# Moving operand sums, layer norm, an output projection and softmax reductions in a fused attention and gated-MLP kernel

## The chip, the cores and the metric

The kernel runs on one core of one Trainium2 chip. A core has five engines with a queue each: TensorE (PE in the profile, with its weight loads as PEld), VectorE (DVE), ScalarE (ACT), GpSimd (POOL) and SyncE (SP, used here only to issue loads). Each engine takes its instructions strictly in the order of its queue, and semaphores tie the engines together. The metric is the device time of one execution in microseconds (us); smaller is better.

## What is computed

For a sequence of 2048 rows of width 1024, with 32 heads of 32, a window of 8 keys at a distance of 2 rows each, and an inner MLP width of 3584:

```python
xn = layernorm(x)                                  # over the 1024 columns, no weights
q, k, v = split(xn @ wqkv)                         # 32 heads of 32
logits[s, w] = q[s] . k[s - 2 w] * 32 ** -0.5      # w = 0..7, masked where s - 2 w < 0
o[s] = sum_w softmax_w(logits)[s, w] * v[s - 2 w]
s = o @ wo
g = silu((silu(xn @ w1) * (xn @ w3)) @ w2)
out = x + s * g
```

Inputs and output are bfloat16.

## The kernel before, in words

The sequence is cut into four chunks of 512 rows (c = 0..3) and two blocks of two chunks (b = 0, 1). For a block the program says, in this order: the q, k, v projection of the first chunk (`qkv`), four sums of the block's normed input (`xn_sums`), most of the MLP's first half (`mlp_up`), the attention of the first chunk, `qkv` of the second chunk, the rest of `mlp_up`, the attention of the second chunk, and `down_wo` (the MLP's second half, with the layer norm of the next block's chunks in its middle, and the output projection `wo` of both chunks at its end).

**Products by seven instead of eight.** The MLP's products are done as 2x2 block products with seven multiplications (a Strassen-Winograd scheme), so operands must be added and subtracted first. `mlp_up` runs over 14 steps (`fb`, 256 columns of w1 and w3 each), and a step has seven products for each of two 128-column halves, of 4 matmuls each: 56 matmuls of 128x512. The weight sums of a step (`st`, lines 289 to 292) are made by VectorE in block 0, written to DRAM (`s_dram`, line 293) and only loaded again in block 1. Likewise the sums of w2's four quarters (`w2_sums`, lines 346 to 355) are made once, written to `t_dram`, and loaded in `down_wo`. Before, all 14 `w2_sums` are said ahead of `mlp_up(0)`; they work in place, in the two halves of the space of the second chunk's q (`qo[:, 1]`), which is free until `qkv(1)`.

**Inside a step of `mlp_up`** the order of products is a11 (into `ua`), s1 (into `ue`), a12, s2 (into `ub`), s4 (into `ue`), s3 (into `ub`), and last a22 into `ub`, which is put off as `tail` and issued behind the next step's first two products. VectorE adds `ue` to a saved sum (line 327) and `ub` to another (line 332); line 332 reads the bank `ub` into which the tail then accumulates, so the tail's matmuls wait for it. Lines 340 and 343 multiply up and gate.

**Who sets the order.** The kernel is written with a framework that takes the program order as priority, works out each engine's queue ahead of time with a model of how long everything takes, and puts in all semaphores. `tc.high_priority()` lifts instructions above the others. So VectorE's queue is a fixed mixture of operand sums, evacuations of PSUM and pieces of attention; whatever stands in front must finish (or get its data) before what is behind can start. Pools hand out buffers by tag: `r8` has six buffers of 8 KiB per partition, which hold the x tiles, the weight tiles `wt`, the sums `st` and `wot`; `att` three; `k2` eight; PSUM eight banks.

**Attention of a chunk** is all on VectorE but the exponential: 8 x (two products of q and shifted k, lines 210 to 214), a rearranging transfer by 16 DMAs of POOL's queue (line 218), three additions, maximum, subtraction, exponential, sum, reciprocal, product (lines 222 to 235), a rearranging transfer back (line 238), then 16 products with shifted v and 14 additions (lines 246 to 261), which leave the result in `qo`. A halo of 16 columns of kT and vT is copied by POOL at the start of the next `qkv` (lines 182 and 183), and only then may the new k and v be written.

**`down_wo`** does seven products of 4 x 14 matmuls, with operand sums on VectorE in place (lines 396, 397, 406, 417). The layer norm of the next block's chunks (`ln_norm`, lines 139 to 156, VectorE statistics with the square root on ScalarE) and its transposes on TensorE (`ln_tp`) stand between its products (lines 435 and 444). The gate `gt` lies in the memory of `xs`. At the end the output projections of both chunks follow, 64 matmuls each; VectorE evacuates each bank by lines 469 and 470 without priority.

Of the kernel before, what the change touches and what calls it, by code (L numbers as in the profile page):

```python
# [16 lines left out]
def kernel(  # L17
# [106 lines left out]
    def bank(name):  # L124
        return psum.tile([P, CH], FP32, tag="mm", name=name)
# [31 lines left out]

    def ln_tp(c, st, xt4):
        for kh in range(2):
            tp = bank(f"tp{c}_{st}_{kh}")  # L160
            for k in range(KH):
                kt = kh * KH + k
                nc.tensor.matmul(
                    tp[:, k * P:(k + 1) * P], lhsT=xt4[:, st, kt * P:(kt + 1) * P], rhs=ident[:],
                    start=(k == 0), stop=(k == KH - 1), skip_group_check=True,
                )
            nc.scalar.copy(
                out=xT[:, c % 2, kh * KH:(kh + 1) * KH, st * P:(st + 1) * P],
                in_=tp[:].rearrange("p (k t) -> p k t", k=KH),
            )  # L170
# [31 lines left out]

    def attention(c):
# [23 lines left out]
        mx = small.tile([P, P], FP32, tag="mx", bufs=1)  # L227
        nc.vector.tensor_reduce(out=mx[:], in_=z[:].rearrange("p w s -> p s w"), axis=AX.X, op=ALU.max)
        nc.vector.tensor_sub(z[:], z[:], mx[:].unsqueeze(1).to_broadcast([P, W, P]))
        nc.scalar.activation(out=z[:], in_=z[:], func=ACTF.Exp, scale=scale)  # L230
        ssum = small.tile([P, P], FP32, tag="ssum", bufs=1)
        nc.vector.tensor_reduce(out=ssum[:], in_=z[:].rearrange("p w s -> p s w"), axis=AX.X, op=ALU.add)
        nc.vector.reciprocal(out=ssum[:], in_=ssum[:])
        pb = att.tile([P, W, P], BF16, tag="a4", name=f"pb{c}")
        nc.vector.tensor_mul(pb[:], z[:], ssum[:].unsqueeze(1).to_broadcast([P, W, P]))  # L235
# [27 lines left out]
    def xn_sums():  # L263

        k_1, k_2 = slice(0, KH), slice(KH, KT)
        nc.vector.tensor_sub(xs[:, 0], xT[:, 1, k_1, :], xT[:, 0, k_1, :])
        nc.vector.tensor_sub(xs[:, 1], xT[:, 1, k_2, :], xs[:, 0])
        nc.vector.tensor_sub(xs[:, 2], xT[:, 1, k_2, :], xT[:, 1, k_1, :])
        nc.vector.tensor_sub(xs[:, 3], xT[:, 0, k_2, :], xs[:, 1])
# [10 lines left out]

    def mlp_up(b, fbs):
        for fb in fbs:
            fc = slice(fb * 256, (fb + 1) * 256)
            wt = r8.tile([P, 2, KT, 2 * P], BF16, tag="r8")
            st = r8.tile([P, 4, KH, 2 * P], FP16, tag="r8")
            nc.sync.dma_start(out=wt[:, 0], in_=w1_r[:, :, fc])
            if b == 0:
                nc.sync.dma_start(out=wt[:, 1], in_=w3_r[:, :, fc])
                nc.vector.tensor_add(st[:, 0], wt[:, 1, 0:KH], wt[:, 1, KH:KT])  # L289
                nc.vector.tensor_sub(st[:, 1], st[:, 0], wt[:, 0, 0:KH])  # L290
                nc.vector.tensor_sub(st[:, 2], wt[:, 0, 0:KH], wt[:, 1, 0:KH])
                nc.vector.tensor_sub(st[:, 3], wt[:, 0, KH:KT], st[:, 1])  # L292
                nc.gpsimd.dma_start(out=s_dram[fb], in_=st[:])  # L293
            else:
                nc.sync.dma_start(out=st[:], in_=s_dram[fb])
                nc.sync.dma_start(out=wt[:, 1, KH:KT], in_=w3_r[:, KH:KT, fc])
# [27 lines left out]
            for i in I:  # L324
                mm_prod(pe[i], s4[i], b22, False)
                with hp():
                    nc.vector.tensor_add(su2[i][:], pe[i][:], su2[i][:])
            sg2 = []
            for i in I:
                mm_prod(pb[i], s3[i], t3, False)  # L330
                with hp():
                    nc.vector.tensor_add(h_sb[:, fl[i], CH:BL], pb[i][:], sp5[i][:])  # L332
                    sg2.append(k2.tile([P, CH], BF16, tag="k2", name=f"sg2{b}_{fl[i]}"))
                    nc.scalar.activation(out=sg2[i][:], in_=su2[i][:], func=ACTF.Silu)

# [9 lines left out]

    def w2_sums(i):

        bq = qo[:, 1].rearrange("p (u q) n -> p u q n", u=2)[:, i % 2]
        tq = bq.bitcast(FP16)
        nc.sync.dma_start(out=bq.rearrange("p (a c) n -> p a c n", a=2), in_=w2_q[:, i])  # L350
        nc.vector.tensor_sub(tq[:, 0], bq[:, 1], bq[:, 0])  # L351
        nc.vector.tensor_sub(tq[:, 1], bq[:, 3], bq[:, 1])
        nc.vector.tensor_sub(tq[:, 3], bq[:, 3], tq[:, 0])
        nc.vector.tensor_sub(tq[:, 2], bq[:, 2], tq[:, 3])  # L354
        nc.gpsimd.dma_start(out=t_dram[:, i], in_=tq)  # L355

    T1, T3, T4, T2 = range(4)

    def down_wo(b):
# [20 lines left out]
        def hA(row, fh):  # L380
            return [[h_sb[:, fh * FH + k, gsl[row][g]] for k in range(FH)] for g in G]
# [6 lines left out]
        gt = [xsb[:, 2 * u:2 * u + 2].rearrange("p a k n -> p (a k) n") for u in range(2)]  # L388
# [6 lines left out]
        for g in G:  # L395
            nc.vector.tensor_add(s1t[g], a21[g], a22[g])
            nc.vector.tensor_sub(s3t[g], a11[g], a21[g])
        rhs = rhs_tiles("w", 0, 0)
        lhs = hA(0, 0)
# [4 lines left out]
        for g in G:  # L404
            pb.append(fork(f"db{b}_{g}", pa[g]))
            nc.vector.tensor_sub(s2t[g], s1t[g], a11[g])
# [9 lines left out]
        for g in G:  # L416
            nc.vector.tensor_sub(s4t[g], a12[g], s2t[g])
# [16 lines left out]
        if b + 1 < NB:  # L434
            ln_transpose(2 * b + 2)
# [7 lines left out]
        if b + 1 < NB:  # L443
            ln_transpose(2 * b + 3)
# [7 lines left out]
        wots = []  # L452
        for dh in range(2):
            wot = r8.tile([P, NJ, CH], BF16, tag="r8")
            nc.sync.dma_start(out=wot[:], in_=wo_r[:, :, dh * CH:(dh + 1) * CH])
            wots.append(wot)
        for u in range(2):
            c = 2 * b + u
            for dh in range(2):
                cols = slice(dh * CH, (dh + 1) * CH)  # L460
                for st in range(NST):
                    g0 = (c * NST + st) * P
                    ps = bank(f"s{c}_{dh}_{st}")
                    mm_prod(ps, [qo[:, u, j, st * P:(st + 1) * P] for j in range(NJ)],
                            [wots[dh][:, j, :] for j in range(NJ)], True)
                    x_e = k2.tile([P, 2, CH], BF16, tag="k2")
                    nc.sync.dma_start(out=x_e[:, 0], in_=x_flat[g0:g0 + P, cols])
                    o_t = k2.tile([P, CH], FP32, tag="k2")
                    nc.vector.tensor_mul(o_t[:], ps[:], gt[u][:, dh * NST + st])
                    nc.vector.tensor_add(x_e[:, 1], o_t[:], x_e[:, 0])  # L470
                    nc.scalar.dma_start(out=out_flat[g0:g0 + P, cols], in_=x_e[:, 1])

    cut = (12, 10)
    ln_transpose(0, group=1)
    ln_transpose(1)
    for b in range(NB):
        c0, c1 = 2 * b, 2 * b + 1
        qkv(c0)
        xn_sums()
        if b == 0:  # L480
            for i in range(FH):
                w2_sums(i)
# [7 lines left out]
        down_wo(b)  # L490
# [30 lines left out]
```

## Time and profile before

| | |
|---|---|
| median of 3 runs | 811.35 us (808.3 to 812.58) |
| the profiled execution, whole | 811.54 us |
| its span, first to last instruction | 809.8 us |
| instructions in it | 9377 |
| granted TensorE clock, mean | 0.972 |
| DMA | 146.37 MB, 181 GB/s on average |

The profile is of one execution, so it explains 811.54 us, which is 0.02% from the median. Between the span and the whole lie 1.74 us. TensorE counts as busy while a matmul is in its pipe, so 94% busy does not say that it runs at its peak; that has to be worked out from the number of matmuls and the time of one. The granted clock is a share of full speed, and falls after an idle time.

### The profile page before, as it was taken

Reading aid. Unit: us, or ns where it says so; the run is one execution under the profiler, and the core shown is the slowest. Engines: PE = TensorE matmul, PEld = TensorE weight load, DVE = VectorE, ACT = ScalarE, POOL = GpSimd, SP = SyncE. Lnnn points to the kernel's source line nnn. Section 1 sums busy time; section 2 is a strip of 40 time slices with the busy share of each in tenths; the row PEclk is TensorE's granted clock in tenths of the full one; section 3 lists DMA queues with packets and bytes.
Section 4 is the critical chain, followed back from the end, with each engine's and each line's share of the span. In section 5 each row is a group of like instructions: output and inputs, shape, how many; then the busy total and the mean of one; then the engine's idle time right before and its main releaser. Section 6 shows DMA issues by size and latency. Waiting matters only on the chain.

```text
span 809.8 us, 9377 instructions
## 1 busy us (share of the span) xinstructions
PE 757.9 (94%) x3516; PEld 378.2 (47%) x3516; DVE 621.8 (77%) x845; ACT 291.7 (36%) x494; POOL 122.5 (15%) x172
## 2 busy tenths in 40 slices
PE   5998679999999799996969999999999999999997
PEld 2664234444456444443424664444446644444443
DVE  7458789857779999585798389584895895955976
ACT  4333234435533241227300334565443345311200
POOL 0011010221400503904000000404000004040000
PEclk7999799999999999998988999999999999999999
DMA  9687785666752545565726443847553438465423
GB/s 331 239 285 247 257 263 196 188 168 216 217 199 75 174 152 171 171 170 147 255 91 194 170 151 128 229 131 202 187 175 124 137 136 224 160 177 181 130 64 119
DMA packets 118958, 146.37 MB, mean 181 GB/s; under 512 B 6016, under 2 KB 93568, under 8 KB 115328
## 3 DMA queue, kind: packets, MB, share of 16 engines
q1 hardware_dynamic: 106176, 111.16, 43.7%
q0 software_dynamic: 8128, 30.42, 11.4%
q10 hardware_dynamic: 4608, 4.20, 1.5%
q8 instruction: 27, 0.44, 0.2%
q14 instruction: 19, 0.16, 0.1%
HBM read 111.15 MB, written 26.21 MB: 170 GB/s over the span
## 4 chain that ended last, share of the span: by engine, by line
PE 61%; DVE 20%; DMA 10%; issue 4%; ACT 2%; POOL 2%; SPq 0%; DVEq 0%; POOLq 0%
DMA qo<-in_B_w_dram 4%; DMA wt<-in_B_w_dram 4%; DVE p_t L210 2%; DVE stats L148 2%; DVE B L246 1%; DVE C L246 1%; DVE B L260 1%; POOL vT L183 1%; DVE qo L261 1%; PE db_3_5573 L119 1%; PE db_2_5570 L119 1%; PE db_1_5567 L119 1%; PE db_0_5564 L119 1%; DVE h_sb L332 1%; DMA L_1_2424<-E 1%
## 5 line engine op out<-in xcount | busy, mean ns | idle before, releaser
L119 PEld LDWEIGHTS <-wt 128*128 128x128 bf16 x1440 | 176.7, 123 | 163.7 <-issue 33.8
L119 PEld LDWEIGHTS <-st 128*128 128x128 f16 x896 | 87.7, 98 | 106.1 <-issue 0.5
L119 PEld LDWEIGHTS <-h_sb 128*128 128x128 bf16 (+1 forms) x672 | 65.8, 98 | 78.2 <-issue 1.1
L210 DVE TENSOR_TENSOR p_t<-qo,kT 128x2048 bf16<-128x2048 bf16 x64 | 77.1, 1216 | 27.0 <-ACT kT L201 27.0
L119 PEld LDWEIGHTS <-qo 128*128 128x128 bf16 x256 | 25.7, 100 | 40.4 <-issue 11.7
L212 DVE TENSOR_TENSOR p_t<-p_t 128x2048 bf16<-128x2048 bf16 x32 | 38.9, 1215 | 0.0
L246 DVE TENSOR_TENSOR B<-E,vT 128x2048 bf16<-128x2048 bf16 x32 | 38.6, 1216 | 0.0
L182 POOL COPY kT<-kT 128x128 bf16<-128x128 bf16 x3 | 19.0, 6325 | 122.6 <-DVE p_t L210 122.6
L183 POOL COPY vT<-vT 128x128 bf16<-128x128 bf16 x3 | 13.4, 4471 | 150.0 <-DVE C L246 150.0
L261 DVE TENSOR_TENSOR qo<-qo,B 128x2048 bf16<-128x2048 bf16 x24 | 29.2, 1217 | 0.2
L260 DVE TENSOR_TENSOR B<-B,C 128x2048 bf16<-128x2048 bf16 x24 | 29.2, 1216 | 0.1
L246 DVE TENSOR_TENSOR C<-E,vT 128x2048 bf16<-128x2048 bf16 x24 | 29.2, 1216 | 0.0
L351 DVE TENSOR_TENSOR qo<-qo 128x512 f16<-128x512 bf16 x14 | 5.9, 422 | 28.2 <-DMA qo<-in_B_w_dram 28.2
L470 DVE TENSOR_TENSOR x_e<-o_t,x_e 128x512 bf16<-128x512 f32 x32 | 21.7, 687 | 3.3 <-DMA x_e<-in_A_x_dram 2.8
L355 POOL DMA_DIRECT2D t_dram<-qo x14 | 7.6, 546 | 95.4 <-DVE qo L354 85.1
L213 DVE TENSOR_TENSOR p_t<-p_t 128x1024 bf16<-128x1024 bf16 x32 | 21.9, 684 | 0.2
L293 POOL DMA_DIRECT2D s_dram<-st x14 | 7.6, 544 | 76.5 <-DVE st L292 67.4
L246 DVE TENSOR_TENSOR qo<-E,vT 128x2048 bf16<-128x2048 bf16 x8 | 9.7, 1216 | 9.9 <-DMA E<-pb_5430 9.9
L119 PEld LDWEIGHTS <-xT 128*128 128x128 f16 x112 | 10.9, 98 | 13.2
L289 DVE TENSOR_TENSOR st<-wt 128x1024 f16<-128x1024 bf16 x14 | 9.6, 685 | 9.8 <-DMA wt<-in_B_w_dram 9.8
L201 ACT CAST qo<-qkv_0_0_3418 128x512 bf16<-128x512 f32 x1 | 0.6, 586 | 39.9 <-DMA out_dram<-x_e 39.9
L238 POOL DMA_DIRECT2D E<-pb_5430 x16 | 9.2, 580 | 32.3 <-DVE pb_5430 L235 30.6
(1312 smaller groups left out, 1598.1 us busy)
## 6 DMA issues: line engine op xcount, KB each, us to landing
wt<-in_A_wqkv_dram SPq DMA_DIRECT2D x24, 1024.0 KB, 5.8
wt<-in_B_w_dram SPq DMA_DIRECT2D x42, 512.0 KB, 4.8
s_dram<-st POOLq DMA_DIRECT2D x14, 1024.0 KB, 7.1
wt<-t_dram SPq DMA_DIRECT2D x16, 896.0 KB, 5.3
st<-s_dram SPq DMA_DIRECT2D x14, 1024.0 KB, 5.6
wt<-in_B_w_dram SPq DMA_DIRECT2D x12, 896.0 KB, 5.2
qo<-in_B_w_dram SPq DMA_DIRECT2D x14, 512.0 KB, 4.6
t_dram<-qo POOLq DMA_DIRECT2D x14, 512.0 KB, 4.0
```

The costliest lines, as they stand in the source:

```text
L119: nc.tensor.matmul(ps[:], lhsT=lhs[k], rhs=rhs[k], start=(first and k == 0), stop=(k == n - 1), skip_group_check=not first,)
L148: nc.vector.bn_stats(out=stats[:, h, :], in_=xt4[:, st, h * 512:(h + 1) * 512])
L182: nc.gpsimd.tensor_copy(out=kT[:, :, 0:HALO], in_=kT[:, :, CH:CH + HALO])
L183: nc.gpsimd.tensor_copy(out=vT[:, :, 0:HALO], in_=vT[:, :, CH:CH + HALO])
L210: nc.vector.tensor_mul(p_t[:], qT[:, jh * 4:jh * 4 + 4, :], kT[:, jh * 4:jh * 4 + 4, o:o + CH])
L212: nc.vector.tensor_add(pr[0][:], pr[0][:], pr[1][:])
L213: nc.vector.tensor_add(pr[0][:, 0:2, :], pr[0][:, 0:2, :], pr[0][:, 2:4, :])
L246: nc.vector.tensor_mul(dst, E[:, w, :].unsqueeze(1).to_broadcast([P, 4, CH]), vT[:, js, o:o + CH])
L260: nc.vector.tensor_add(B[:], B[:], C[:])
L261: nc.vector.tensor_add(A, A, B[:])
L289: nc.vector.tensor_add(st[:, 0], wt[:, 1, 0:KH], wt[:, 1, KH:KT])
L470: nc.vector.tensor_add(x_e[:, 1], o_t[:], x_e[:, 0])
```

## The change

- `mlp_up` loads the tiles of step fb + 1 before the matmuls of step fb (`up_load`). In block 0 the weight sums of step fb + 1 (`w_sums`) are queued on VectorE behind step fb's second line-327 addition ("m"), by an ordering constraint (`tc.issue_after`).
- `w2_sums(fb)` moves into step fb of block 0, queued behind that step's last line-332 addition ("t"); its quarters are loaded a step earlier (`w2_load`), into one buffer of the pool `r8` instead of q's space.
- The layer norm of chunks 2 and 3 is said at the start of `mlp_down` and runs on ScalarE (`ln_norm_act`: mean by a copy with accumulation, sum of squares, root, then scale and shift), except for two tiny VectorE instructions. The transposes stay between the same products.
- `wo` becomes a function of one chunk. A block's second `wo` comes behind the `qkv` of the next block's first chunk (at the end, behind the first `wo`). It loads its weights for each chunk. Its evacuations get priority.
- The maximum and the sum over the 8 window positions become trees of three pairwise operations.
- `xn_sums` and the operand sums of the down half get priority, and block 0's first part has 11 steps instead of 12.

```diff
+    def ln_norm_act(c, sts, xt4):
+        n = len(sts)
+        v = small.tile([P, 4, n], FP32, tag="v")
+        for i, st in enumerate(sts):
...
+            nc.sync.dma_start(out=x_t, in_=x_flat[g * P:(g + 1) * P, :])
+            junk = k2.tile([P, D], BF16, tag="k2", name=f"junk{c}_{st}")
+            nc.scalar.activation(out=junk[:], in_=x_t, func=ACTF.Copy, scale=-1.0 / D, accum_out=v[:, 0, i:i + 1])
+            nc.scalar.activation(out=junk[:], in_=x_t, func=ACTF.Square, bias=v[:, 0, i:i + 1], accum_out=v[:, 1, i:i + 1])
+        nc.scalar.activation(out=v[:, 2], in_=v[:, 1], func=ACTF.Sqrt, bias=eps_t[:], scale=1.0 / D)
+        with tc.high_priority():
+            nc.vector.reciprocal(out=v[:, 2], in_=v[:, 2])
+            nc.vector.tensor_mul(v[:, 3], v[:, 0], v[:, 2])
+        for i, st in enumerate(sts):
+            x_t = xt4[:, st, :]
+            nc.scalar.activation(out=x_t, in_=x_t, func=ACTF.Identity, bias=v[:, 3, i:i + 1], scale=v[:, 2, i:i + 1])
+    def tree(t, z, op):
+        op(t[:], z[:, 0:4, :], z[:, 4:8, :])
+        op(t[:, 0:2, :], t[:, 0:2, :], t[:, 2:4, :])
+        op(t[:, 0:1, :], t[:, 0:1, :], t[:, 1:2, :])
...
-        nc.vector.tensor_reduce(out=mx[:], in_=z[:].rearrange("p w s -> p s w"), axis=AX.X, op=ALU.max)
+        zm = att.tile([P, W // 2, P], FP32, tag="a4", name=f"zm{c}")
+        tree(zm, z, nc.vector.tensor_max)
...
-        nc.vector.tensor_reduce(out=ssum[:], in_=z[:].rearrange("p w s -> p s w"), axis=AX.X, op=ALU.add)
+        zs = att.tile([P, W // 2, P], FP32, tag="a4", name=f"zs{c}")
+        tree(zs, z, nc.vector.tensor_add)
...
+    def up_load(b, fb):
...
+        wt = r8.tile([P, 2, KT, 2 * P], BF16, tag="r8", name=f"w{b}_{fb}")
+        st = r8.tile([P, 4, KH, 2 * P], FP16, tag="r8", name=f"st{b}_{fb}")
+        tiles[b, fb] = wt, st
+        nc.sync.dma_start(out=wt[:, 0], in_=w1_r[:, :, fc])
+        if b == 0:
+            nc.sync.dma_start(out=wt[:, 1], in_=w3_r[:, :, fc])
...
+    def behind(key):
+        return tc.issue_after(anchor[key].ins) if key in anchor else nullcontext()
+    def w_sums(fb):
+        wt, st = tiles[0, fb]
+        with behind(("m", fb - 1)):
+            nc.vector.tensor_add(st[:, 0], wt[:, 1, 0:KH], wt[:, 1, KH:KT])
+            nc.vector.tensor_sub(st[:, 1], st[:, 0], wt[:, 0, 0:KH])
+            nc.vector.tensor_sub(st[:, 2], wt[:, 0, 0:KH], wt[:, 1, 0:KH])
+            nc.vector.tensor_sub(st[:, 3], wt[:, 0, KH:KT], st[:, 1])
+        nc.gpsimd.dma_start(out=s_dram[fb], in_=st[:])
...
+            if fb + 1 < FB:
+                up_load(b, fb + 1)
...
+            if b == 0:
+                anchor["m", fb] = m
+                if fb + 1 < FB:
+                    w_sums(fb + 1)
...
+            if b == 0:
+                anchor["t", fb] = m
+                w2_sums(fb)
+                if fb + 1 < FB:
+                    w2_load(fb + 1)
...
+            tiles["t"] = r8.tile([P, 2, 4, CH], BF16, tag="r8", name="w2q")
...
     def w2_sums(i):
-        bq = qo[:, 1].rearrange("p (u q) n -> p u q n", u=2)[:, i % 2]
+        bq = w2_quarters(i)
...
+        for c in range(2 * b + 2, 2 * b + 4 if b + 1 < NB else 0):
+            xn.append(r8.tile([P, NST, D], BF16, tag="r8", name=f"x{c}"))
+            ln_norm_act(c, range(NST), xn[-1])
...
-        if b + 1 < NB:
-            ln_transpose(2 * b + 2)
+        for st in range(NST if b + 1 < NB else 0):
+            ln_tp(2 * b + 2, st, xn[0])
...
+    def wo(c):
...
+                with tc.high_priority():
+                    nc.vector.tensor_mul(o_t[:], ps[:], gt[:, dh * NST + st])
                     nc.vector.tensor_add(x_e[:, 1], o_t[:], x_e[:, 0])
                     nc.scalar.dma_start(out=out_flat[g0:g0 + P, cols], in_=x_e[:, 1])
-    cut = (12, 10)
+    cut = (11, 10)
     ln_transpose(0, group=1)
     ln_transpose(1)
     for b in range(NB):
         c0, c1 = 2 * b, 2 * b + 1
         qkv(c0)
+        if b == 0:
+            w2_load(0)
+        else:
+            wo(c0 - 1)
         xn_sums()
-        if b == 0:
-            for i in range(FH):
-                w2_sums(i)
         mlp_up(b, range(cut[b]))
         attention(c0)
         flush()
...
         attention(c1)
-        down_wo(b)
+        mlp_down(b)
+        wo(c0)
+    wo(2 * NB - 1)
```

112 lines of the change are left out of this document (58 added, 54 removed).

## The prediction

> **What bounds the kernel now.** First the stages. I cut the span at the first matmul of each stage in the timeline of TensorE and asked for the busy time of each engine in each stretch (columns: from:to, length, then busy us and instructions by engine; after them the granted clock, the DMA share and GB/s). The chain that ended last gives a dense product, and the timeline two transposes in a row.
>
> ```profile
> 64.41:233.25 168.84, 150.96 (x673) 66.52 (x672) 130.48 (x215) 72.83 (x125) 29.91 (x52) 0.96 0.69 220
> 233.25:278.72 45.47, 41.60 (x193) 27.50 (x192) 45.29 (x46) 10.01 (x18) 11.09 (x3) 1.00 0.37 115
> 278.72:303.55 24.83, 24.49 (x113) 10.95 (x112) 22.87 (x32) 14.82 (x27) 0.39 (x1) 1.00 0.55 198
> 303.55:401.94 98.39, 90.61 (x458) 42.37 (x456) 75.20 (x101) 34.90 (x55) 35.76 (x33) 0.97 0.58 179
> 401.94:440.40 38.46, 30.80 (x130) 13.25 (x129) 34.51 (x41) 0.60 (x1) 1.74 (x1) 0.87 0.44 147
> 440.40:805.40 365.00, 364.77 (x1689) 182.51 (x1687) 274.83 (x338) 133.88 (x222) 38.28 (x66) 1.00 0.51 159
> ```
> ```profile
> 696.20 3.02 PE da_1_5519 L119 x14
> ```
> ```profile
> 387.67 0.39 PE L163 MATMUL tp_0_0_3040<-ident,x_3023 128*128 128x128 bf16 x4
> 387.89 0.39 PE L163 MATMUL tp_0_1_3046<-ident,x_3023 128*128 128x128 bf16 x4
> ```
>
> 14 matmuls in 3.02 us are 0.2157 us each; four transposes start 0.22 us after the last four. With the counts of the code, dense work and loss by stage are:
>
> - `mlp_up(0)`, 12 steps of 56: 672 x 0.2157 = 145.0 of 168.84, loss **23.8**.
> - `qkv(1)` with its end, 192: 41.4 of 45.47, loss **4.1**.
> - last two steps, 112: 24.2 of 24.83, loss 0.7.
> - down half of block 0, 392 and 64 transposes: 84.6 + 3.5 = 88.1 of 98.39, loss **10.3**.
> - both `wo` of block 0, 128: 27.6 of 38.46, loss **10.9**.
> - all of block 1, 1688: 364.1 of 365.00, loss 0.9.
>
> So block 1 already runs dense, and everything to be had lies between 64 and 440 us: 49.8 us. Next, who is waited for: the waits of TensorE, longest first, then the longest of VectorE.
>
> ```profile
> PE ub_0_664 L119 <- DVE h_sb L332: 9.4, 1, 9.4
> PE tp_0_0_2891 L163 <- DVE dsu_0_2684 L441: 7.5, 1, 7.5
> PE s_0_1_3307 L119 <- DVE o_t L469: 4.9, 1, 4.9
> PE ua_24_2186 L119 <- ACT vT L201: 3.9, 1, 3.9
> PE ub_2_747 L119 <- DVE h_sb L332: 3.1, 1, 3.1
> PE s_0_2_3322 L119 <- DVE o_t L469: 2.7, 1, 2.7
> ```
> ```profile
> DVE qo L351 <- DMA qo<-in_B_w_dram: 28.2, 10, 9.1
> ```
>
> TensorE waits for VectorE each time but one, and VectorE's own longest wait is the quarters of w2. Now the worst stall in order of time: TensorE, VectorE, SP's queue.
>
> ```profile
> 73.90 1.03 PE L119 MATMUL ub_1_666<-xs,st 128*128 128x512 f16 x4
> ...
> 87.82 1.86 PE L119 MATMUL ub_0_664<-xs,wt 128*128 128x512 f16 x4 [9.44 <-DVE h_sb L332]
> 89.48 1.91 PE L119 MATMUL ub_1_666<-xs,wt 128*128 128x512 f16 x4
> ```
> ```profile
> 83.41 0.68 DVE L289 TENSOR_TENSOR st<-wt 128x1024 f16<-128x1024 bf16 x1
> ...
> 85.22 0.68 DVE L327 TENSOR_TENSOR us_0_686<-ue_0_654,us_0_686 128x512 f32<-128x512 f32 x1
> ...
> 87.09 0.68 DVE L332 TENSOR_TENSOR h_sb<-ub_0_664,us_0_668 128x512 bf16<-128x512 f32 x1
> ...
> 88.62 0.41 DVE L343 TENSOR_TENSOR h_sb<-h_sb,sg_0_709 128x512 bf16<-128x512 bf16 x1
> ```
> ```profile
> 77.32 0.73 SPq L288 DMA_DIRECT2D wt<-in_B_w_dram  x1
> ```
>
> The bank that line 327 needs was done before 73.90, yet VectorE adds it at 85.22: in its fixed order a sum of a later step (line 289, on a load issued only at 77.32) and the quarters stand in front. Line 332 is late, the tail waits 9.44 us, and then the clock is down: four matmuls in 1.66 us instead of 0.86. The `ub` waits of this stage add to some 17 us; the rest of the 23.8 is such slow restarts.
>
> **The change part by part.**
>
> *Sums a step behind their loads.* Prices, from the page's groups:
>
> ```profile
> L289 DVE TENSOR_TENSOR st<-wt 128x1024 f16<-128x1024 bf16 x14 | 9.6, 685 | 9.8 <-DMA wt<-in_B_w_dram 9.8
> ```
> ```profile
> L351 DVE TENSOR_TENSOR qo<-qo 128x512 f16<-128x512 bf16 x14 | 5.9, 422 | 28.2 <-DMA qo<-in_B_w_dram 28.2
> ```
> ```profile
> L210 DVE TENSOR_TENSOR p_t<-qo,kT 128x2048 bf16<-128x2048 bf16 x64 | 77.1, 1216 | 27.0 <-ACT kT L201 27.0
> ```
>
> VectorE does in a step of 56 x 0.2157 = 12.1 us: 4 x 0.685 of weight sums, 4 x 0.422 of quarters, six evacuations of 0.68 (lines 327, 332, 340) and two of 0.41: 9.3 us. No operation goes; waits on DMA do. Every load now has a step to land, against 4 to 7 us measured. The new wait is the anchor: behind it stand the sums, then whatever follows on VectorE, and TensorE waits for them. Line 327's pair is due at 40 matmuls, 8.6 us, and done at 10.0; the first sum at 10.7; the next step uses it after its first product, at 12.1 + 1.7 = 13.8. Slack 3.1 us, and one piece of attention (1.2 us) fits in. I keep 3 us of the 23.8 for late steps: **-20.8** (ends 0 and -23.8). The extra queue entries (SP: the same loads, a step earlier; POOL: both writes of a step, 0.5 us each) hide under the step; if a `t_dram` write holds up the next quarter load on SP, it holds the weight loads behind it too, with a step's reserve.
>
> *The buffer for the quarters* takes one of six `r8` places throughout `mlp_up(0)`, and the prefetched step 11 takes two during `qkv(1)`: three remain for its six weight tiles.
>
> ```profile
> wt<-in_A_wqkv_dram SPq DMA_DIRECT2D x24, 1024.0 KB, 5.8
> ```
>
> At worst each of the three pairs waits 5.8 us, 17.4 in all; at best the first halves of eight products (32 x 0.2157 = 6.9 us) cover each load, as the order of TensorE already mixes banks where an operand is late. I take **+2**, near the low end.
>
> *Layer norm on ScalarE.* In the down half:
>
> ```profile
> 365.68 1.87 DVE L148 BATCH_NORM_STATS2 stats<-x_3023 128x6 f32<-128x512 bf16 x3
> ...
> 375.68 0.67 DVE L441 TENSOR_TENSOR dsu_0_2684<-de_0_2798,dsu_0_2684 128x512 f32<-128x512 f32 x1
> ```
> ```profile
> 360.10 1.06 ACT L230 ACTIVATE z_2441<-z_2441 128x1024 f32<-128x1024 f32 x1 [4.00 <-DVE z_2441 L229]
> ```
>
> Line 441 frees the bank that the first transpose needs, and it stands behind statistics and scalings of chunk 3. Those 16 statistics of 0.62 us, and the scalings, go: about 15 us of VectorE. ScalarE gets 24 passes of 1,024 elements at 1.06 us, 25.4 us, on top of 34.9 in 98.39: it fits, though a fork may wait one pass. The two small VectorE operations wait for ScalarE's root; behind them are sums due a product (12 us) later. With 7.5 us of wait and its slow restart I take **-8.0** of 10.3 (ends -1, if another VectorE piece stands in front, and -10.3).
>
> *Second `wo` behind the next `qkv`.* The last addition of chunk 1's attention:
>
> ```profile
> 426.18 1.21 DVE L261 TENSOR_TENSOR qo<-qo,B 128x2048 bf16<-128x2048 bf16 x1
> ```
>
> TensorE reached `wo` at 401.94 and had to stop for this. Now 13.8 us of the first `wo` and 41.4 of `qkv(2)` come first: attention may end 55 us behind the down half, where it ended 25.5 behind. Even if TensorE gains 29 us and attention none, it is in time. Priority on lines 469 and 470 frees the banks. Four more weight loads of 1 MB land under these 55 us. The gate lies in `xs`, so two of `xn_sums` wait for the second `wo`; they are needed 8.6 us later. **-9.9** of 10.9 (ends -3, only the shorter wait, and -10.9).
>
> *Trees.*
>
> ```profile
> 193.36 1.91 DVE L228 TENSOR_REDUCE mx<-z_1837 128x128 f32<-128x1024 f32 x1
> ```
>
> 512, 256 and 128 elements at line 327's 0.68 per 512 are some 1.2 us, so 0.7 less, eight times, on VectorE where it is not last: 0.
>
> *`qkv(1)`*: its 4.1 us come from the halo copy:
>
> ```profile
> 267.63 10.42 POOL L183 COPY vT<-vT 128x128 bf16<-128x128 bf16 x1 [45.15 <-DVE C L246]
> ```
> ```profile
> 149.28 1.24 POOL L182 COPY kT<-kT 128x128 bf16<-128x128 bf16 x1 [5.01 <-DVE p_t L210]
> ```
>
> It starts when attention has read v last, and the same copy took 1.24 us once and 10.42 here, with VectorE busy without a break. One step less ahead of `qkv(1)` takes 12 us of cover from chunk 0's attention, the stalls that go take 21 more, and VectorE no longer idles 28 us: about even. I take 0 (ends -4.1 and +10). [...]
>
> Sum: -20.8 + 2 - 8.0 - 9.9 = -36.7, from 811.54: **774.8 us**. Start, block 1 and end stay.
>
> **The rivals.**
>
> 1. *`qkv(1)` becomes the bound.* Chunk 0's attention ends late and the copy holds the new v: 4.1 us now plus up to 10, with the buffers' stall in the same place, say +10: 785. For it: VectorE is busy 45.29 of 45.47 us there. Against: 15 us of cover come from waits that vanish.
> 2. *The steps don't gain.* If VectorE's lateness in `mlp_up(0)` is its load and not the DMA, the 23.8 us stay and only the down half and `wo` gain: 811.5 - 17.9 + 2 = 796. For: 9.3 of 12.1 us plus attention. Against: steps 3 to 11 already run nearly without waits.
> 3. *Slower: the anchor.* If VectorE reaches line 327 over 3.1 us late in every step, its sums arrive after their first use. At 6.2 us late, each of 13 steps loses 3.1 us and 1.6 of slow restart (two products at 1.66 for 0.86): 13 x 4.7 = 61, so 775 + 61 = 836; it turns the sign from 3.2 us of loss per step. For: line 327 was 12 us late at 85.22. Against: that was the order around missing data.
> 4. *No effect*, within 0.5%: would need gains and one of these to cancel.
>
> **How the numbers follow.** Chances: forecast (764 to 783) 0.66, rival 1 0.17, rival 2 0.07, rival 3 0.08, rival 4 0.02. The range takes in the forecast and rival 1: from 764, where all but a few of the 49.8 us are gone, to 790. A measurement here can tell 0.5% from no change: faster by more 0.90, within 0.02, slower 0.08.
>
> **What would show it.** Right: TensorE's waits on line 332 under 1 us each, none of 7 us at the first transposes, `wo` of chunk 1 without waits on line 469, and 12.1 us from step to step. Wrong: waits on `st` in every step (rival 3), on vT over 8 us at the end of `qkv(1)` or on its weight tiles (rival 1), line 332 as before (rival 2).

## The result and the profile after

The changed kernel takes **776.69 us** (median of 4 runs, 776.28 to 779.28) against 811.47 us of the kernel before on the same chip: a ratio of 0.9584, 95% interval 0.955 to 0.9618. The prediction was 774.8 us, 764 to 790. The profiled execution took 779.28 us (span 777.5), the slowest of the four, so the stages below explain 811.54 - 779.28 = 32.3 us of the 34.8 us between the medians. One of the four runs of the kernel without anchors (below) took 2049.62 us against 787.95 to 789.75 us of the other three and is left out of everything that follows; it has no profile, and why it was slow is not known.

The stages of the changed kernel, cut as in the prediction at the first matmul of each, but `qkv(1)` from the end of the products before it, so that its first wait counts as its own (from:to, length, busy us and instructions of PE, PEld, DVE, ACT, POOL, granted clock, DMA share, GB/s):

```profile
65.21:198.77 133.56, 132.66 (x606) 60.05 (x615) 117.64 (x208) 69.78 (x115) 29.84 (x53) 1.00 0.79 249
198.77:247.63 48.86, 43.53 (x190) 27.55 (x194) 48.59 (x50) 13.48 (x23) 2.25 (x3) 0.97 0.61 203
247.63:284.54 36.91, 36.50 (x166) 16.26 (x168) 33.52 (x55) 19.83 (x34) 2.12 (x4) 1.00 0.63 213
284.54:374.26 89.72, 88.77 (x452) 41.96 (x456) 44.87 (x60) 57.70 (x90) 21.38 (x34) 1.00 0.69 210
374.26:443.33 69.07, 68.70 (x314) 40.08 (x320) 65.12 (x71) 14.14 (x25) 1.13 (x1) 1.00 0.61 199
443.33:773.35 330.02, 324.94 (x1472) 155.65 (x1495) 255.60 (x326) 120.06 (x198) 38.33 (x66) 0.99 0.53 164
```

Some matmul records are missing from this trace (606 of 616 in the first stage), so the matmuls are counted from the code. With 0.2157 us for a matmul, and 616, 192, 168, 392 (and 3.5 us of transposes), 320 and 1496 matmuls, the loss of each stage is its length less its dense work:

| stage | loss before | predicted | loss after |
|---|---|---|---|
| `mlp_up(0)`, first part | 23.8 | 3 | 0.7 |
| `qkv(1)` | 4.1 | 6.1 | 7.4 |
| last steps of `mlp_up(0)` | 0.7 | 0.7 | 0.7 |
| down half of block 0 | 10.3 | 2.3 | 1.7 |
| both `wo` (after: with `qkv(2)` between) | 10.9 | 1.0 | 0.0 |
| block 1 | 0.9 | 0.9 | 7.3 |

The stalls of the kernel before are gone, more fully than forecast; 15 us of loss stand in two places, one of them quite new. The waits of TensorE in the changed kernel show both, and nothing else of weight (line, what it waits for: us in total, times, longest; the rows left out belong to the start):

```profile
PE qkv_0_0_1831 L119 <- DMA wt<-in_A_wqkv_dram: 4.4, 1, 4.4
PE ua_0_3677 L119 <- ACT ub_0_3697 L130: 3.4, 1, 3.4
...
PE da_0_2585 L119 <- DMA wt<-in_B_w_dram: 0.7, 1, 0.7
PE qkv_2_0_1999 L119 <- DMA wt<-in_A_wqkv_dram: 0.4, 1, 0.4
PE ub_18_4504 L119 <- DVE h_sb L380: 0.4, 1, 0.4
```

Line 380 (332 before) no longer costs more than 0.4 us at a time, and the first transposes and the bank of `wo` are not in the list. What is there instead:

**`qkv(1)` waits for its weights.** The queue of SP, in order of time:

```profile
184.36 0.37 SPq L406 DMA_DIRECT2D w2q<-in_B_w_dram  x1
184.83 0.41 SPq L313 DMA_DIRECT2D w_11_1560<-in_B_w_dram  x1
185.68 0.37 SPq L315 DMA_DIRECT2D w_11_1560<-in_B_w_dram  x1
196.70 0.37 SPq L406 DMA_DIRECT2D w2q<-in_B_w_dram  x1
197.18 2.15 SPq L206 DMA_DIRECT2D wt<-in_A_wqkv_dram  x3
```

TensorE was through with the eleven steps at 198.77, and the first weight tile was only asked for at 197.18. In front of it stood the load of the next quarters of w2 (line 406), which waited for a write to `t_dram` that landed at 196.64 and was issued 11 us after the load ahead of it.

**The first step of block 1 waits for ScalarE.** The step in order of time, across the engines:

```profile
439.58 10.00 ACTq L540 DMA_DIRECT2D out_dram<-x_e  x7
...
445.92 1.03 PE L119 MATMUL ue_1_3692<-xs,st_0_3668 128*128 128x512 f16 x4
...
448.67 0.69 DVE L538 TENSOR_TENSOR o_t<-s_1_3_3648,xs 128x512 f32<-128x512 f32 x1
...
449.68 0.57 ACT L130 COPY ub_0_3697<-ua_0_3677 128x512 f32<-128x512 f32 x1 [19.37 <-DVE o_t L538]
...
450.30 1.86 PE L119 MATMUL ua_0_3677<-xT,w_0_3667 128*128 128x512 bf16 x4 [3.35 <-ACT ub_0_3697 L130]
...
451.96 1.91 PE L119 MATMUL ua_1_3682<-xT,w_0_3667 128*128 128x512 bf16 x4
```

The output writes (line 540) are issued on ScalarE's queue, inside the block that the change gave priority. Each waits for VectorE's addition to the second `wo`, and ScalarE's copy of `ua` (line 130), for which TensorE stops, stands behind them. ScalarE's engine stood idle for 19.37 us, and TensorE needed its copy from 446.95 on. The four matmuls after the wait take 1.86 us instead of 1.03, and so on for some products.

### The profile page after: what moved, and what is told of

It reads as the page before. It is cut to its first block, busy times and chain, and to the rows that moved or that the text cites. A ratio compares the mean times of both kernels' runs of the same rounds, so it can differ in the third digit from the quotient of the medians.

```text
span 777.5 us, 9339 instructions
## 1 busy us (share of the span) xinstructions
PE 750.1 (96%) x3457; PEld 377.0 (48%) x3516; DVE 602.0 (77%) x829; ACT 319.6 (41%) x531; POOL 97.2 (12%) x172
## 4 chain that ended last, share of the span: by engine, by line
PE 90%; DVE 4%; DMA 4%; issue 1%; ACT 1%; SPq 0%; ACTq 0%; DVEq 0%
DMA wt<-in_A_wqkv_dram 2%; PE db_0_2645 L119 1%; PE db_2_5575 L119 1%; PE db_3_2654 L119 1%; PE db_1_5572 L119 1%; PE db_2_2651 L119 1%; PE db_3_5578 L119 1%; PE db_0_5569 L119 1%; PE db_1_2648 L119 1%; DVE stats L148 1%; PE da_2_5539 L119 1%; PE da_0_5509 L119 1%; PE de_1_2876 L119 1%; PE de_2_5819 L119 1%; PE de_1_5800 L119 1%
## 5 line engine op out<-in xcount | busy, mean ns | idle before, releaser
L119 PEld LDWEIGHTS <-wt 128*128 128x128 bf16 x768 | 110.3, 144 | 64.9 <-DMA wt<-in_A_wqkv_dram 6.5
L201 POOL COPY vT<-vT 128x128 bf16<-128x128 bf16 x3 | 3.5, 1170 | 152.6 <-DVE C L269 152.6
L417 POOL DMA_DIRECT2D t_dram<-w2q x14 | 7.6, 541 | 55.7 <-DVE w2q L416 55.7
L261 POOL DMA_DIRECT2D E<-pb_5434 x16 | 9.2, 580 | 36.4 <-DVE pb_5434 L258 34.0
L237 DVE TENSOR_TENSOR E<-p_t 128x512 bf16<-128x512 bf16 x32 | 13.4, 420 | 0.1
L261 POOL DMA_DIRECT2D E<-pb_4658 x16 | 9.2, 598 | 27.6 <-DVE pb_4658 L258 26.6
L261 POOL DMA_DIRECT2D E<-pb_2460 x16 | 9.2, 580 | 27.1 <-DVE pb_2460 L258 27.1
L241 POOL DMA_DIRECT2D L_0_5402<-E x8 | 4.6, 584 | 53.3 <-DVE E L237 52.2
L200 POOL COPY kT<-kT 128x128 bf16<-128x128 bf16 x3 | 3.0, 1017 | 65.0 <-DVE p_t L233 54.5
```

The source lines that it names most:

```text
L119: nc.tensor.matmul(ps[:], lhsT=lhs[k], rhs=rhs[k], start=(first and k == 0), stop=(k == n - 1), skip_group_check=not first,)
L237: nc.vector.tensor_add(E[:, w, :], pr[0][:, 0, :], pr[0][:, 1, :])
L261: nc.gpsimd.dma_start(out=E[r:P:NR, :, sq * P:(sq + 1) * P], in_=pb[sq * 32:(sq + 1) * 32, :, :],)
```

## The experiments

Times are medians of four runs (three without anchors, ten for the doubled sums); the ratio is to the kernel before on the same chip. Losses of the stages are worked out as above. The first is all from the first step to the last of `mlp_up(0)` with `qkv(1)` between, since part of a wait in `qkv(1)` shows up in the step after it; matmuls of the next stage that slip in ahead of a boundary are counted where they belong, and block 1 ends with the last matmul. Losses belong to the profiled execution, which is not always near the median: it took 779.28 us in the changed kernel, 776.32 with layer norm back, and 804.66 with `wo` alone.

| kernel | us | ratio, 95% | `mlp_up(0)`, `qkv(1)` | down | `wo` | block 1 |
|---|---|---|---|---|---|---|
| before | 811.5 | | 28.6 | 10.3 | 10.9 | 0.9 |
| after | 776.7 | 0.955 to 0.962 | 8.8 | 1.7 | 0.0 | 7.3 |
| no anchors | 789.3 | 0.968 to 0.977 | 18.9 | 0.9 | 0.0 | 8.7 |
| quarters ahead | 789.1 | 0.969 to 0.975 | 24.0 | 0.8 | 0.0 | 4.0 |
| layer norm back | 778.5 | 0.956 to 0.962 | 8.1 | 1.9 | 0.0 | 6.4 |
| `wo` back | 804.4 | 0.988 to 0.994 | 9.7 | 1.3 | 33.1 | 0.9 |
| quarters in q | 774.6 | 0.951 to 0.957 | 5.4 | 1.4 | 0.0 | 7.2 |
| late quarter load | 777.2 | 0.956 to 0.961 | 8.1 | 1.2 | 0.0 | 5.9 |
| writes on POOL | 780.7 | 0.960 to 0.965 | 10.0 | 1.3 | 0.0 | 5.9 |
| quarters in q and writes on POOL | 776.0 | 0.954 to 0.959 | 5.4 | 1.5 | 0.0 | 4.5 |
| layer norm alone | 800.5 | 0.985 to 0.989 | 25.2 | 1.4 | 10.5 | 0.9 |
| `wo` alone | 800.8 | 0.985 to 0.989 | 29.5 | 11.5 | 0.0 | 3.1 |
| sums doubled | 811.5 | 0.998 to 1.002 | 41.0 | 1.7 | 0.0 | 8.2 |
| best | 768.2 | 0.946 to 0.949 | 5.4 | 1.7 | 0.0 | 0.5 |

### What in the steps brought the gain

**No anchors.** The sums stay a step behind their loads in the program, without the ordering constraints.

```diff
     def behind(key):
-        return tc.issue_after(anchor[key].ins) if key in anchor else nullcontext()
+        return nullcontext()
```

> The two anchors go (weight sums behind line 371's pair, quarters behind line 397's), the loads stay a step ahead. Theory A: the loads a step ahead are what removed the stalls of mlp_up(0), since then no sum waits for data; VectorE's order changes little: 777 to 780 us, waits of TensorE on the evacuations of mlp_up(0) under 3 us in sum. Theory B: the place in VectorE's order that the anchor fixes is what counts, sums run too early in front of line 371 again: 787 to 800, and the evacuations of line 380 show waits of several us.

789.3 us, as theory B had it. Waits on line 380 are back (first row, TensorE's waits: 9.4 us in total, 5 of them, the longest 6.1), and VectorE stands on the quarters again (second row, VectorE's waits):

```profile
PE ub L119 <- DVE h_sb L380: 9.4, 5, 6.1
```
```profile
DVE w2q L413 <- DMA w2q<-in_B_w_dram: 27.5, 7, 13.2
```

So a load a step ahead is not enough. Left to itself, the order made ahead of time puts the sums of the next step, those of two steps' quarters and pieces of attention in front of line 371 again. In the first step its bank is done at 73.3, and VectorE, busy without a break since 66.2, comes to it at 82.59:

```profile
82.59 1.28 DVE L371 TENSOR_TENSOR us<-ue,us 128x512 f32<-128x512 f32 x2
```

VectorE starts late, since most of its wait for quarters falls ahead of the steps. The anchors are worth 12.7 us of the gain. In this run the end of `qkv(1)` waits for the halo copy again (3.5 us, on vT), so the 12.7 us are not those of the steps alone.

**Quarters ahead.** The weight sums are as in the change, but all sums of w2's quarters said ahead of `mlp_up(0)`, in q's second half, as in the kernel before.

```diff
-        if b == 0:
-            w2_load(0)
...
+        if b == 0:
+            for i in range(FH):
+                w2_load(i)
+                w2_sums(i)
```

> All quarters of w2 are loaded and summed in a row ahead of mlp_up(0), in q's second half, as before the change; the weight sums stay as changed, and the quarters hold no r8 place. Theory A: VectorE stands again on the quarters (over 20 us of its waits on qo from the DMA) and TensorE with it: 12 to 24 us come back in mlp_up(0), and up to 6 of qkv(1)'s 7.4 us of loss go: 781 to 794. Theory B: the quarters were not what stopped the steps, the weight sums alone were: qkv(1) gains its 6 us and nothing comes back: 770 to 774.

789.1 us, theory A. VectorE waits 25.4 us for the quarters, and TensorE for VectorE (waits of TensorE, then of VectorE):

```profile
PE ub L119 <- DVE h_sb L380: 14.4, 4, 10.7
```
```profile
DVE qo L408 <- DMA qo<-in_B_w_dram: 25.4, 8, 8.7
```

The worst stall of the kernel before (9.44 us on the first tail) is thus that of the quarters: moving the weight sums alone leaves it, at 10.7 us. In the same run `qkv(1)` loses nothing, which points at the quarters' buffer or load for the 7.4 us there.

**Sums doubled.** The four weight sums of each step are done twice.

```diff
-            nc.vector.tensor_add(st[:, 0], wt[:, 1, 0:KH], wt[:, 1, KH:KT])
+            for _ in range(2):
+                nc.vector.tensor_add(st[:, 0], wt[:, 1, 0:KH], wt[:, 1, KH:KT])
...
```

> The weight sums of every step of mlp_up(0) are done twice: 2.7 us more of VectorE behind the anchor in each of 14 steps. Theory A (the prediction's slack of 3.1 us): the sums still come in time, waits on st stay under 1 us a step; attention and what hangs on it comes later instead, 777 to 790. Theory B (the third rival's mechanism): there is no slack, TensorE waits on st in most steps and restarts slowly, 1 to 4.7 us a step: 790 to 836.

811.5 us, theory B, and the whole gain of the change is gone: the steps and `qkv(1)` now lose 41.0 us instead of 28.6, which takes up what the down half and `wo` still gain. TensorE waits for the first sum in 12 steps, 2.2 us each (its waits, then its timeline):

```profile
PE ue L119 <- DVE st L327: 26.5, 12, 3.5
```
```profile
114.10 1.90 PE L119 MATMUL ue<-xs,st 128*128 128x512 f16 x8 [2.20 <-DVE st L327]
...
128.98 3.12 PE L119 MATMUL ue<-xs,st 128*128 128x512 f16 x8 [2.62 <-DVE st L327]
```

The repeat of the first sum, for which TensorE waits, ends 3.6 to 5.5 us after the first one and not 2.7, since VectorE does other pieces between the sums. So this run shows that the sums are on TensorE's path, but not how large the slack was. The changed kernel shows that directly (VectorE, then TensorE):

```profile
111.99 0.69 DVE L326 TENSOR_TENSOR st_4_854<-w_4_853 128x1024 f16<-128x1024 bf16 x1
```
```profile
111.95 1.03 PE L119 MATMUL ua_8_958<-xT,w_4_853 128*128 128x512 bf16 x4
...
113.68 1.03 PE L119 MATMUL ue_8_968<-xs,st_4_854 128*128 128x512 f16 x4
```

The sum is done at 112.68 and used at 113.68. A step before, the same pair stands at 101.46 and 101.59. From step to step the slack is 0.1 to 1.9 us, not 3.1.

### Layer norm and the second `wo`, undone and alone

**Layer norm back** on VectorE, between the products of the down half, in the changed kernel.

```diff
-            ln_norm_act(c, range(NST), xn[-1])
...
-        for st in range(NST if b + 1 < NB else 0):
-            ln_tp(2 * b + 2, st, xn[0])
+        if b + 1 < NB:
+            ln_transpose(2 * b + 2)
```

> Layer norm of chunks 2 and 3 goes back to VectorE, behind the products of the down half as before. Theory A (the term -8.0 of the prediction): the bank that the first transposes need is late again, and the down half of block 0 loses 8 to 10 us instead of 1.6: 784 to 787. Theory B: layer norm was only in front because VectorE was late for other reasons that are gone now: 776 to 779, no wait of TensorE over 2 us at the transposes.

778.5 us, theory B; with intervals that overlap it can't be told from the changed kernel. TensorE waits 1.0 us at the first transposes. VectorE's timeline there:

```profile
345.17 1.27 DVE L148 BATCH_NORM_STATS2 stats<-x 128x6 f32<-128x512 bf16 x2
...
347.55 0.68 DVE L507 TENSOR_TENSOR dsu<-de,dsu 128x512 f32<-128x512 f32 x1
```

The statistics are still there, but the last of them in front of the first `dsu` addition (line 507, 441 before) end at 346.44, before TensorE has to stop at 347.25. In the kernel before TensorE stopped at 368.89, and statistics and scalings went on until 375.

**Layer norm alone** on ScalarE, in the kernel before (its edit is the `ln_norm_act` part of the change).

```diff
+            ln_norm_act(c, range(NST), xn[-1])
...
-        if b + 1 < NB:
-            ln_transpose(2 * b + 2)
+        for st in range(NST if b + 1 < NB else 0):
+            ln_tp(2 * b + 2, st, xn[0])
```

> The kernel before, with one part of the change alone: layer norm of chunks 2 and 3 on ScalarE. Theory A (the term -8.0 of the prediction, which holds on the kernel before even though undoing it in the changed kernel cost nothing): the down half of block 0 loses 1 to 3 us instead of 10.3: 802 to 805. Theory B: VectorE's lateness there comes from what was queued up ahead, layer norm only happened to stand in front: the wait at the first transposes stays over 4 us, or what the down half gains comes back as a longer wait for attention at the second wo: 808 to 812.

800.5 us, theory A's mechanism, 1.5 us below its range: the down half loses 1.4 us instead of 10.3. (Another 3.4 us came in the stages ahead of it; what from is not known.) The wait for attention at `wo` stays:

```profile
PE s L119 <- DVE o_t L491: 7.7, 2, 4.9
```

So on the kernel before layer norm was the cause, and in the changed kernel it is not needed any more: there some other part of the change removes the same wait. Which one (the operand sums of the down half got priority too) was not separated.

**`wo` back**: the second `wo` of a block directly behind the first.

```diff
-        else:
-            wo(c0 - 1)
...
         wo(c0)
-    wo(2 * NB - 1)
+        wo(c1)
```

> The second wo of a block directly behind the first again. Theory A (the term -9.9): chunk 1's attention ends long after the down half (pv runs to 426 us in the changed kernel, the down half ends at 374), so the second wo waits for it: 11 to 25 us of loss ahead of block 1, less the 6.3 us that the first step of mlp_up(1) loses now because ScalarE's copies stand behind the output writes of the second wo: 781 to 796. Theory B: attention speeds up when nothing stands in front of it, and the second wo finds it done: 770 to 773.

804.4 us: theory A's mechanism, at a price above its range. TensorE reaches the second `wo` at 387.6 and waits 28.9 us in two pieces, for the last additions of chunk 1's attention:

```profile
411.55 9.20 PE L119 MATMUL s<-wot,qo 128*128 128x512 bf16 x32 [23.98 <-DVE qo L284]
425.67 1.91 PE L119 MATMUL s<-wot,qo 128*128 128x512 bf16 x5 [4.92 <-DVE qo L284]
```

Attention ends at 425.6, against 427.4 in the kernel before: up to there VectorE has gained next to nothing by the change, only TensorE has. Without the moved `wo` most of what the steps and the down half gain is given back here; all the rest of the change is worth 7 us. Block 1 loses 0.9, as in the kernel before, so its new loss belongs to the place of the second `wo`.

**`wo` alone**: the same move, with its priorities and that of `xn_sums`, in the kernel before.

```diff
+        if b > 0:
+            wo(c0 - 1)
         xn_sums()
...
+                with tc.high_priority():
                     nc.vector.tensor_mul(o_t[:], ps[:], gt[:, dh * NST + st])
```

> The kernel before, with one part of the change alone: the second wo of a block behind the next qkv, its evacuations and the sums of xn with priority. Theory A (the term -9.9): both wo lose under 1 us instead of 10.9; the first step of mlp_up(1) then loses 6 to 7 us as it does in the changed kernel, so 805 to 808, and 801 if that loss belongs to the denser kernel only. Theory B: the move is worth nothing on the kernel before, its attention ends in time anyway with less in front: 810 to 812.

800.8 us, theory A with the lower of its two prices: 10.9 us gone at `wo`, and the wait at the transposes untouched. Block 1 loses 3.1 instead of 0.9, less than in the changed kernel:

```profile
PE tp L163 <- DVE dsu L444: 7.9, 1, 7.9
...
PE ua L119 <- ACT ub L130: 1.8, 1, 1.8
```

### The two losses that are new

**Quarters in q**: for steps 0 to 10 the quarters go through q's second half, and the quarter load of step 11 is said at that step.

```diff
+            if b == 0 and fb == cut[0]:
+                w2_load(fb)
...
-                if fb + 1 < FB:
+                if fb + 1 < FB and fb + 1 != cut[0]:
                     w2_load(fb + 1)
...
     def w2_quarters(i):
+        if i < cut[0]:
+            return qo[:, 1].rearrange("p (u q) n -> p u q n", u=2)[:, i % 2]
```

> The quarters of w2 for steps 0 to 10 go through q's second half, which is free until qkv(1); only the last three steps use an r8 place, and the quarter load of step 11 is issued at that step. The anchors stay. Theory A: the 7.3 us that qkv(1) loses come from the quarters (place in r8, or their load in front on SP's queue): its loss falls to 0 to 2 us, the rest stays, 770 to 772. Theory B: they come from the prefetched weights of step 11 alone, two of six places whatever the quarters do: qkv(1) loses 5 us or more, 775 to 778.

774.6 us. `qkv(1)` now loses 1.1 us, as theory A has it. But the time is 2.6 us above its range; the steps ahead of `qkv(1)` lose 1.7 us more and those behind it 1.3 (with a wait of 1.3 us on the first sum in either). The weight tiles are now asked for 10 us earlier:

```profile
186.63 28.57 SPq L206 DMA_DIRECT2D wt<-in_A_wqkv_dram  x6
```

**Late quarter load**: the quarters keep their place in `r8`, and only the load of step 11's quarters is said at that step (the first two pieces of the diff above).

> The quarters keep their r8 place, but the load of step 11's quarters, which stands on SP's queue in front of the weight tiles of qkv(1) and waits for a write to t_dram, is issued at step 11. Theory A (queue): qkv(1) loses 0 to 2 us, as in the run with the quarters in q, 770 to 772. Theory B (place): three places for six tiles, the load of the first tiles still waits for places, and the 4.4 us wait on wt stays: 775 to 778.

777.2 us, with the 3.7 us wait on `wt`. But the edit did not reach its object: the framework put a quarter load into the same place of SP's queue.

```profile
196.14 0.37 SPq L408 DMA_DIRECT2D w2q<-in_B_w_dram  x1
196.61 2.73 SPq L206 DMA_DIRECT2D wt<-in_A_wqkv_dram  x3
```

This run is in effect the changed kernel once more, and does not count for theory B. That the quarters are the cause is shown; whether it is their place in `r8` or their load ahead on SP's queue was not separated by a run. The changed kernel's own trace points to the queue for the 4.4 us that TensorE waited (TensorE, then SP's queue):

```profile
188.79 1.03 PE L119 MATMUL ub_19_1485<-xs,w_9_1358 128*128 128x512 f16 x4
...
197.91 1.03 PE L119 MATMUL ub_21_1586<-xs,w_10_1459 128*128 128x512 f16 x4
```
```profile
198.96 0.37 SPq L206 DMA_DIRECT2D wt<-in_A_wqkv_dram  x1
```

The third weight tile of `qkv(1)` is asked for at 198.96, just as the last product that reads step 10's weights ends (198.94), so it took their place. The last product with step 9's weights ended at 189.82, so a place for the first tile was free 7.4 us before that tile was asked for, at 197.18 behind the quarter load. Which tile got which place is inferred from these times.

**Writes on POOL**: the output writes of `wo` are issued on GpSimd's queue.

```diff
-                    nc.scalar.dma_start(out=out_flat[g0:g0 + P, cols], in_=x_e[:, 1])
+                    nc.gpsimd.dma_start(out=out_flat[g0:g0 + P, cols], in_=x_e[:, 1])
```

> Only the queue of the eight output writes of each wo changes, from ScalarE's to GpSimd's. Theory A: the first step of mlp_up(1) loses 6 to 7 us because ScalarE's copies (line 130) stand behind output writes that wait for VectorE's additions: without them block 1 loses under 1.5 us, 770 to 771. Theory B: ScalarE's copies are late for another reason (passes of layer norm, VectorE's priority pieces): the 3.4 us wait on line 130 stays, 776 to 778.

780.7 us, neither: the wait on line 130 is gone, and block 1 still loses 5.9 us. The wait has moved to VectorE:

```profile
456.56 0.67 DVE L371 TENSOR_TENSOR us<-ue,us 128x512 f32<-128x512 f32 x1
...
459.62 3.44 PE L119 MATMUL ub<-xs,w 128*128 128x512 f16 x8 [2.76 <-DVE h_sb L380]
```

VectorE, at the end of sixteen evacuations of the second `wo`, does six pieces of chunk 2's logits (the first at 449.35) before the addition of line 371. And the end is later: the last write is issued at 772.98 and the span ends at 779.4, 8 us behind TensorE where ScalarE's queue had 4.

**Quarters in q and writes on POOL** together:

> Quarters in q's second half for steps 0 to 10, and output writes on GpSimd's queue. If the two losses are independent: 776.7 - 6 - 6.3 = 764 us, 763 to 767. If one of them only moves the wait to the next late engine (as the undone wo did, where attention took back what the steps had gained): 769 to 773.

776.0 us, above either expectation. Block 1 still loses 4.5 us and `qkv(1)` 1.5, and the end is 4 us later, as with the writes on GpSimd's queue alone.

**Best**: quarters in q; the last four output writes of block 0's second `wo` behind ScalarE's copies of the first step, by an ordering constraint on ScalarE's own queue; and the logits of chunk 2, from the third window on, behind that step's line-380 additions.

```diff
-                nc.vector.tensor_mul(p_t[:], qT[:, jh * 4:jh * 4 + 4, :], kT[:, jh * 4:jh * 4 + 4, o:o + CH])
+                with behind(("l", c) if w >= 2 else None):
+                    nc.vector.tensor_mul(p_t[:], qT[:, jh * 4:jh * 4 + 4, :], kT[:, jh * 4:jh * 4 + 4, o:o + CH])
...
+            while writes:
+                o, x = writes.pop(0)
+                with tc.issue_after(last[0].ins):
+                    nc.scalar.dma_start(out=o, in_=x)
...
+            if b == 1 and fb == 0:
+                anchor["l", 2] = m
...
+                    if c == 1 and dh == 1:
+                        writes.append((out_flat[g0:g0 + P, cols], x_e[:, 1]))
+                    else:
                         nc.scalar.dma_start(out=out_flat[g0:g0 + P, cols], in_=x_e[:, 1])
```

> The changed kernel with the quarters in q's second half for steps 0 to 10 (774.6 alone), the last four output writes of block 0's second wo said behind ScalarE's copies of the first step of mlp_up(1), and from the third window on the logits of chunk 2 behind that step's sums on VectorE. Theory A: ScalarE's queue and VectorE's order together make the 7 us that block 1 loses: its loss falls under 2 us, 767 to 770. Theory B: the wait moves on once more, as it did when the writes went to GpSimd: 773 to 776.

768.15 us (767.86 to 768.45), 0.9473 of the kernel before (0.9458 to 0.9488): theory A. ScalarE's copy starts right behind its product (ScalarE's row), and block 1 runs dense (windows, `qkv(1)` and block 1):

```profile
439.68 0.57 ACT L130 COPY ub<-ua 128x512 f32<-128x512 f32 x1 [14.13 <-PE ua L119]
```
```profile
199.04:241.91 42.87, 41.66 (x193) 27.43 (x192) 42.63 (x43) 12.32 (x23) 2.25 (x3) 1.00 0.59 203
...
438.57:761.55 322.98, 322.98 (x1497) 155.03 (x1495) 256.74 (x326) 119.91 (x198) 38.20 (x66) 1.00 0.54 166
```

Its interval and that of the changed kernel don't overlap, so this version beats both.

## Why the prediction was right, and where it was wrong

The time came out 1.9 us above the forecast, within its range. Three gains were a little larger than forecast (4.0 us in all, in the profiled execution), and two losses were too small or missing (7.7 us). That these errors partly cancel is luck. All four signs that it named for being right are in the trace (line 332's successor at most 0.4 us, no long wait at the transposes, none at `wo` on VectorE, 12.1 us from step to step), and so is one that it named for the first rival, the wait on the weight tiles of `qkv(1)`.

- *Sums a step behind their loads, -20.8.* Measured -23.1. The mechanism was right (VectorE standing on data in a fixed order), and both halves of it are needed: without the anchors 12.7 us come back, with the quarters ahead 12.4. But the step "slack 3.1 us" was wrong. It put line 327's pair at 40 matmuls; the tail of the step before comes first, so it is 48, 10.4 us, which leaves 1.4, and in the trace the sum is done 0.1 to 1.9 us ahead of its use. The third rival lay much nearer than its price made it look: four sums more on VectorE per step and the whole gain is gone. Its turning point of 3.2 us per step is also too high, since 36.7 us over 13 steps are 2.8.
- *Buffer for the quarters, +2, and the halo copy, 0.* The wait on the weight tiles came, at 7.4 us with its slow restart, and the halo copy's 4.1 us went: +3.3 in all. Of the first rival the one half happened and the other did the opposite: that the copy could hold it up by 10 us more was an estimate, and the copy took 1.13 us. The prediction had seen that a quarter load could hold up the weight loads behind it on SP, and took a step's reserve for granted there; it is the same place.
- *Layer norm, -8.0.* Measured -8.7 in its stage, and -8.9 alone on the kernel before. The size and the cause were right for the kernel before. As a part of the whole change it is worth nothing that can be measured: the terms of the sum were priced one by one on the kernel before, and this one overlaps with the rest.
- *Second `wo`, -9.9.* Measured -10.9, in the change and alone. It was worth more than that: undone in the changed kernel it costs 27.7 us, because attention ends at 425.6 us there (427.4 in the kernel before), while TensorE is done with the down half 28 us earlier. The prediction's sentence that the move would be in time "even if TensorE gains 29 us and attention none" describes what happened; that the other gains depend on it was not said.
- *"Start, block 1 and end stay."* This step failed, by 6.4 us at block 1. The prediction counted priority on lines 469 and 470 as freeing the banks and did not follow the third instruction of that block, the output write on ScalarE's queue, nor what is queued behind it: the copies of the next step. The best version shows that this write and the order of VectorE behind it together are that loss (0.5 us are left); their shares were not separated.
- *Trees, 0.* Not tried alone, and neither were the priorities of the operand sums and the step that moved behind `qkv(1)`, for which the sum has no term.

## What to carry to other kernels

A term priced on the kernel before is only good for that kernel: undo each part in the changed kernel as well, since one part may be worth nothing (layer norm, 0 to 2 us) and another nearly everything (`wo`, 28 us of 35). When instructions are given priority or moved, follow every instruction in them to its queue, DMA issues too, and name what waits behind; here a write that nobody waits for stopped TensorE for 3.4 us through ScalarE. An order made ahead of time is held by constraints where it matters (12.7 us here), not by loading earlier, and a wait that is removed on one queue (ScalarE) may stand on the next (VectorE, 2.8 us) until both are put in order.

## What was not expected of the hardware

*The halo copy.* The first rival had GpSimd's copy, 10.42 us in the kernel before, hold up `qkv(1)` by up to 10 us more; it took 1.13 us, with VectorE as busy in `qkv(1)` as before (48.59 of 48.86 us, before 45.29 of 45.47). The rows of the changed kernel, GpSimd's and VectorE's:

```profile
235.30 1.13 POOL L201 COPY vT<-vT 128x128 bf16<-128x128 bf16 x1 [31.48 <-DVE C L269]
```
```profile
235.06 1.22 DVE L233 TENSOR_TENSOR p_t<-qo,kT 128x2048 bf16<-128x2048 bf16 x1
236.19 1.31 DVE L283 TENSOR_TENSOR B<-B,C 128x2048 bf16<-128x2048 bf16 x1
```

and VectorE's of the kernel before, where the copy ran from 267.63 to 278.05:

```profile
276.68 1.22 DVE L212 TENSOR_TENSOR p_t<-p_t 128x2048 bf16<-128x2048 bf16 x1
277.93 0.69 DVE L213 TENSOR_TENSOR p_t<-p_t 128x1024 bf16<-128x1024 bf16 x1
```

VectorE's instructions of this size usually start 1.14 us apart. The copy of before ends at 278.05, 0.12 us behind the first start that is later, 1.25 us after the one in front; the copy after ends at 236.43, during one instruction that is stretched to 1.31. Two more long copies end in the same way: in the kernel before, one of 17.44 us ended at 335.26, and VectorE's unbroken run at 335.10; with layer norm alone, one of 10.42 us ended at 274.35, and VectorE started at 274.22, 1.24 us after the start in front. So these three copies end 0.12 to 0.16 us behind a late start of VectorE or the end of its run, and the busy share doesn't tell the copy of 10.42 us from that of 1.13. That the length of the unbroken run decides is the author's reading of these rows and was not tried.

*Slow restarts don't follow from the length of the wait alone.* In the kernels before and after, and up to 470 us in the runs with layer norm alone, with `wo` alone and with the sums doubled, for products of 128x512, TensorE's next eight matmuls take 1.9 us after each wait of 1.4 to 1.8 us, and 2.89 us or more after each wait of 2.6 us and more whose next eight the rows tell apart, but for one. That one is the wait of 3.87 us in the kernel before, followed by 1.89 us at a granted clock of 1.00 (278.72 to 280.61); with layer norm alone the same wait for vT is also 3.87 us, and the eight take 3.44. After the wait of 9.44 us of the kernel before the clock was 0.50 (87.82 to 91.40). Between lie both: with the sums doubled, a wait of 2.20 us was followed by 1.90 us (at 114.10, above), and one of 2.21 us by 2.81 us (at 97.95).
